# Another hand-written order for a linear-attention and MLP kernel on one core

## The chip, the cores and the metric

The kernel runs on one core of one Trainium2 chip. The metric is device time in microseconds (us) of one execution, lower is better. TensorE is called PE here, VectorE DVE, ScalarE ACT, GpSimd POOL and the sync engine SP, as in the profile.

## The reference

Two parts follow each other. The first is attention with decay over blocks of tokens, for 4 batches, 8 heads, 768 tokens and head dimension 64; the second is an MLP on its output, 3072 tokens by 512.

```python
# attention, per batch and head, block after block
intra = einsum('bhic,bhjc->bhij', qb, kb) * Dmask      # lam ** (i - j) for i >= j
intra = einsum('bhij,bhjd->bhid', intra, vb)
inter = einsum('bhid,bhde->bhie', qb * lam_pow, kv_state)
out[:, :, sl] = intra + inter
kv_state = lam_block * kv_state + einsum('bhsd,bhse->bhde', kb * rev_pow, vb)
# MLP, d_model 512, d_ff 2048
h = x @ w_in
g = where(h >= 1, h, where(h <= -1, 0, (h + 1) ** 2 / 4))
return g @ w_out
```

## The kernel before

The 3072 tokens are cut into eight stripes, `STRIPES` on line 28: per batch two pieces, of 4 and 2 blocks of 128 tokens in the first batch and of 3 and 3 in the others. Stripes are numbered 0 to 7. In each, the eight heads are worked on as four pairs, 0 to 3. Nothing is scheduled by a planner at run time or at build time: the kernel is one loop over the words of the string `ORDER` (lines 32 to 74), and each word emits a few instructions. Each engine runs its own instructions strictly in the order in which the words stand, and waits in place where an operand or a buffer isn't ready. So the list sets which instruction waits behind which, on five engines and on two queues that issue transfers: SP's for q, k, v and the results, POOL's for the weights.

The words, with stripe `s` and head pair `p` as the first two digits:

- `L s half c`: load one half of the heads of q, k or v of a stripe (SP, lines 159 to 165). Stripe 0 is loaded in quarters, two heads at a time. `W0` to `W3` load four column blocks of the first weight (line 234), `W4` to `W7` four row blocks of the second (line 238), both on POOL's queue, where the numbers are turned to bf16. `@X` after either makes its first transfer wait until the load `X` has landed.
- `k`, `q`, `v` with a last letter: the decayed k and q and the cast of v, from f32 to bf16 (lines 294 to 319). The last letter is the engine: `a` ACT, `g` POOL, `d` DVE. A k on POOL or ACT is two instructions, on DVE one.
- `T`, `Q`: transposes of k and q, on PE for stripes 0 to 3 (line 343), by a transfer on SP for stripes 4 to 7 (line 335). `t`, `u`: ACT copies them out.
- `S`: scores on PE, `s`: mask on DVE. `R`: products of k and v on PE, `r`: state update on DVE. `b`: the last state of stripe 0 copied into a block-diagonal tile for stripe 1; `z`: decayed k copied into a tile with zero columns. `O`: output on PE (it needs the `s` and the `r` of its pair, in stripe 1 also its `b`), `o`: ACT casts it out. For stripes 4 to 7 `X` transposes it by a transfer on SP.
- `P s n`: one of 16 column blocks of the first matmul (line 594), `K`: the same for blocks 0 to 2 of stripe 0, k-slice by k-slice (line 608); `h`: Relu on ACT (line 617). `A s a`: the rest of the activation on DVE, three instructions over four blocks (lines 574 to 576). `Y s m a`: a quarter of the second matmul for 128 tokens (line 626), which needs `A s a` and weight block `W(4+a)`. `y` copies the result, `U` stores it, `Z72` does all of that for the last 128 tokens (line 646).
- `J`: the zero columns of the tiles `vc`, `kz` and `bd` are cleared on POOL (lines 263 and 265). `E`: a table for the state of stripe 0 on POOL. `B`: mask tables. `G`: zero columns of the tiles of stripes 4 and 5. `D n`: n matmuls of the identity on PE, which no result uses (line 582).

The buffers for q, k and v hold two stripes each, so a load of stripe s waits for the casts of stripe s - 2. Five tiles hold decayed k and q (`kq`).

The order of the start in the list before, engine by engine: SP issues q, k, v of stripe 0 in the order q0 k0 k2 k1 q1 k3 v0 q2 q3 v1 v2 v3, then L10q. POOL does J, k02, E, q03, W0, v02, W1, W2, W3, q11, q10, W4. L10v, L10k and what follows on SP waits for W1 to land. The main loop:

```python
for word in order(NS):
    word, _, dep = word.partition("@")
    ...
    if dep:
        after(dmas[word][0], dmas[dep][-1])
```

Of the kernel before, what the change touches and what calls it, by code (L numbers as in the profile page):

```python
# [38 lines left out]
P09 h08 u10 k13d P0d k11a W6 h0a z13d h09 T10 P0c q13g L20q@W4 b10d T11 v11a t10 P0b S10 s10
z11a W7 z12d P0e t11 h0c R11 Q13 S11 D1 P0f L20v h0b r11 h0d T13 b12a q12d h0f s11 A01 h0e Q12  # L40
T12 A02 t13 Y000 v10a Y020 Y010 Y030 u13 L21q u12 Y031 R10 r10 L30q t12 Y011 Y001 Y021 A03 v12a
k23g Y022 Y012 k21d O11 S12 Y032 v13a R12 o11 s12 Y033 q21g Y023 q20g R13 Y013 k20a r13 r12 S13
O12 y02 s13 o12 Y002 y01 q23g q22g O10 O13 Y003 z21a L30k y03 o10 o13 Q20 P12 P11 u20 T20 h12
P13 t20 Q21 k22d T21 h11 v21d y00 z20d v20d R20 P10 P18 S20 P15 h10 h13 u21 r20 t21 P17 k30g s20
Q22 P19 h18 T22 A10 S21 h19 q30d u22 t22 P16 O20 s21 h17 o20 P14 R21 P1b Q23 T23 h16 L31q h14
z22g k31g P1d S22 L21v@W2 r21 s22 h15 P1e U02 U03 h1b O21 h1d L31k u23 P1a o21 P1c t23 h1a q31g
L31v z23g T30 Q30 q33g P1f u30 v22a Y110 L30v S23 T31 h1c A11 t30 Q31 G40 h1e q32g k32g Y100 R22
A12 t31 Y101 Y111 u31 v23a R23 r22 Y102 h1f s23 r23 S30 O22 O23 s30 k33d z33g o22 Y112 Q32 z30d
z32d T32 z31d v33a v32d v31g A13 o23 t32 G42 u32 P25 T33 h25 P20 S31 v30a P21 Y103 h21 R30 h20
P24 r30 P23 R31 y10 L40k s31 G41 P22 h23 h22 h24 Q33 P26 L40v S32 G43 r31 U00 Y113 h26 P2f P27  # L50
L40q t33 G50 u33 k41d h2f h27 R33 y11 A20 P2e r33 s32 P2b q41g O31 A21 k42a h2e P28 P29 q40g O30
P2a h2b h29 P2c o30 h2a R32 S33 h2c v41d r32 v40a o31 P2d q42g O32 Y200 s33 L50k R41 o32 h28 O33
Y201 o33 P32 P33 L50q h2d k50a h33 v43d A22 P31 k40d h32 q43a Y202 P30 R40 q50g h31 A23 P39 h30
P3a h3a h39 Y210 P36 Y203 T41 A30 h36 P37 y20 T40 S40 s40 h37 Y211 P34 P3e r40 S41 T42 L50v r41
P3d v42g h3e P38 s41 k43g R42 T43 h34 h38 O40 P3b L60q P3c k52g S42 o40 h3d R43 v50g k51a h3b
r42 P35 Y212 s42 r43 S43 O41 P3f s43 Y213 h35 o41 R50 q53a U10 L60k T50 O43 o43 h3c Y220 O42
# [685 lines left out]
```

## Time and profile before

| | us |
|---|---|
| median of 3 runs | 223.96 (223.47 to 226.75) |
| the profiled execution: its time | 224.02 |
| its span in the profile | 222.3 |
| PE busy | 211.4 |
| DVE busy | 155.6 |
| ACT busy | 127.3 |
| POOL busy | 59.7 |

The span is what the profile shows between the first and the last instruction; the 1.7 us beside it lie outside the program's own instructions. A busy PE is a PE with a matmul in flight. In the views quoted below, a timeline row gives the start, the length, the engine, the line, and in brackets how long the engine was idle before it and what ended that. A row of the table by stretches gives for each engine its busy time and, in brackets, its instructions, then PE's granted clock, the share of the transfer engines and GB/s.

### The profile page before, as it was taken

The page shows a single profiled execution, that of the slowest core. Times are in us where ns is not written, and L with a number is a line of the kernel's source. Part 1 is how long each engine was busy: PE and PEld are TensorE (multiplying, and loading weights), DVE is VectorE, ACT ScalarE, POOL GpSimd, SP SyncE. Part 2 cuts the span into 40 slices and gives each one's busy share as a digit, 9 for nine tenths or more (in the row PEclk, how much of TensorE's full clock was granted, in tenths as well). Part 3 has the DMA queues.
Part 4 walks back from the last instruction along what each step waited for, and adds up shares of the span by engine and source line. Part 5 has one row for each costly group of instructions (what it writes and reads, how often), then busy time and mean ns, then how long its engine had stood idle before and what let it go on. Part 6 is the DMA issues. An engine that isn't in the chain of part 4 may idle for free.

```text
span 222.3 us, 4425 instructions
## 1 busy us (share of the span) xinstructions
PE 211.4 (95%) x1675; PEld 121.3 (55%) x1675; DVE 155.6 (70%) x242; ACT 127.3 (57%) x276; POOL 59.7 (27%) x107
## 2 busy tenths in 40 slices
PE   7488999999999899999999999999999999999994
PEld 2245444445875456555654566556565565455543
DVE  6497058964899979898797659948967496307900
ACT  2758499326894668775671776337563564174520
POOL 8446036004592336260353020211610000000000
PEclk9999999999999999999999999999999999999999
DMA  5999999999999999059996999799646103122112
GB/s 124 245 243 152 205 197 177 199 209 232 274 248 228 242 205 196 3 95 221 260 158 163 162 258 255 130 214 201 169 84 165 47 1 86 35 86 104 47 50 94
DMA packets 100629, 35.95 MB, mean 162 GB/s; under 512 B 89216, under 2 KB 97664, under 8 KB 100608
## 3 DMA queue, kind: packets, MB, share of 16 engines
q1 hardware_dynamic: 96384, 31.47, 65.9%
q0 software_dynamic: 4224, 4.19, 12.1%
q8 instruction: 13, 0.21, 0.4%
q14 instruction: 8, 0.07, 0.1%
HBM read 27.27 MB, written 6.29 MB: 151 GB/s over the span
## 4 chain that ended last, share of the span: by engine, by line
PE 75%; DMA 9%; SPq 5%; issue 4%; DVE 4%; POOL 1%; ACT 0%; POOLq 0%; DVEq 0%
PE py L626 33%; PE ph L594 30%; DMA k_nat<-in_k_dram 4%; DMA w_in_sb<-in_moe_w_in_dram 3%; SPq L163 2%; PE ps L367 2%; DMA q_nat<-in_q_dram 2%; SPq L165 2%; PE py L646 2%; PE pk L448 1%; PE po L512 1%; PE ph L608 1%; DVE tt L575 1%; PE po L531 1%; PE pt L343 1%
## 5 line engine op out<-in xcount | busy, mean ns | idle before, releaser
L617 ACT ACTIVATE tt<-ph,one 128x384 bf16<-128x384 f32 (+2 forms) x128 | 70.1, 586 | 39.0 <-PE ph L594 28.9
L594 PE MATMUL ph<-xT,w_in_sb 128*128 128x384 bf16 (+2 forms) x500 | 92.2, 325 | 0.0
L626 PE MATMUL py<-w_out_sb,gT 128*128 128x512 bf16 x368 | 87.4, 379 | 1.2 <-DVE gT L576 1.2
L594 PEld LDWEIGHTS <-w_in_sb 128*128 128x128 bf16 x500 | 46.5, 98 | 29.4 <-issue 0.2
L626 PEld LDWEIGHTS <-gT 128*128 128x128 bf16 x368 | 34.3, 98 | 36.0 <-DVE gT L576 1.6
L574 DVE TENSOR_SCALAR mm<-tt 128x1536 bf16<-128x1536 bf16 (+2 forms) x32 | 19.1, 597 | 22.5 <-ACT tt L617 21.7
L388 DVE TENSOR_TENSOR sc<-ps,mask 128x768 bf16<-128x768 f32 (+1 forms) x28 | 25.6, 915 | 11.7 <-PE ps L367 10.3
L576 DVE TENSOR_TENSOR gT<-tt,mm 128x1536 bf16<-128x1536 bf16 (+2 forms) x32 | 32.7, 1023 | 1.2
L575 DVE TENSOR_TENSOR tt<-tt,mm 128x1536 bf16<-128x1536 bf16 (+2 forms) x32 | 32.1, 1004 | 1.1
L314 POOL TENSOR_SCALAR kq<-k_nat,dec 128x192 bf16<-128x192 f32 (+2 forms) x30 | 20.6, 698 | 29.1 <-PE ps L371 14.7
L634 ACT COPY osb<-py 128x512 f32<-128x512 f32 x23 | 13.5, 586 | 21.2 <-PE py L626 19.9
L319 POOL TENSOR_TENSOR kq<-q_nat,dec 128x384 bf16<-128x384 f32 (+2 forms) x18 | 17.3, 975 | 20.6 <-DMA q_nat<-in_q_dram 9.4
L476 DVE SCALAR_TENSOR_TENSOR sz<-sz,lam_blk,pk 128x128 bf16<-128x128 bf16 x48 | 16.6, 346 | 6.7 <-PE pk L448 5.4
L296 POOL CAST vc<-v_nat 128x384 bf16<-128x384 f32 (+1 forms) x9 | 6.4, 712 | 29.4 <-PE po L531 19.5
L343 PE MATMUL pt<-ident,kq 128*128 128x128 bf16 x96 | 9.4, 220 | 3.5 <-ACT kq L310 2.1
L294 ACT CAST vc<-v_nat 128x384 bf16<-128x384 f32 (+2 forms) x15 | 7.4, 502 | 7.3 <-DMA v_nat<-in_v_dram 7.3
L549 ACT CAST xT<-po 128x384 bf16<-128x384 f32 (+2 forms) x16 | 7.5, 483 | 6.9 <-PE po L526 5.9
L582 PE MATMUL pw<-ident 128*128 128x512 bf16 x31 | 9.8, 432 | 1.4 <-POOL ident masks.py:199 1.4
L343 PEld LDWEIGHTS <-kq 128*128 128x128 bf16 x96 | 6.7, 98 | 7.5 <-ACT kq L310 3.4
L351 ACT COPY kqT<-pt 128x384 bf16<-128x384 bf16 (+2 forms) x16 | 7.8, 490 | 3.4 <-PE pt L343 3.3
L547 ACT CAST xn<-po 128x384 bf16<-128x384 f32 x16 | 7.7, 480 | 3.2 <-PE po L531 3.2
L353 ACT COPY kqT<-pt 128x384 bf16<-128x384 bf16 (+2 forms) x16 | 7.6, 486 | 0.9 <-PE pt L343 0.9
(78 smaller groups left out, 163.6 us busy)
## 6 DMA issues: line engine op xcount, KB each, us to landing
out_dram<-osb SPq DMA_DIRECT2D x23, 256.0 KB, 2.6
q_nat<-in_q_dram SPq DMA_DIRECT2D x18, 256.0 KB, 4.6
k_nat<-in_k_dram SPq DMA_DIRECT2D x24, 128.0 KB, 4.3
v_nat<-in_v_dram SPq DMA_DIRECT2D x24, 128.0 KB, 4.4
k_nat<-in_k_dram SPq DMA_DIRECT2D x12, 256.0 KB, 4.9
v_nat<-in_v_dram SPq DMA_DIRECT2D x12, 256.0 KB, 4.5
w_in_sb<-in_moe_w_in_dram POOLq DMA_DIRECT2D x4, 512.0 KB, 9.1
w_out_sb<-in_moe_w_out_dram POOLq DMA_DIRECT2D x4, 512.0 KB, 8.9
```

Source lines behind the costliest of these rows:

```text
L314: nc.gpsimd.tensor_scalar(dst[:, hi, :, :], src[:, hi, :, :], dec[:, row, 2 * hp + hi:2 * hp + hi + 1], 0.0, AX.mult, AX.add)
L319: (nc.gpsimd if eng == "g" else nc.vector).tensor_tensor(dst, src, decay(row, 2 * hp, C, inner), op=AX.mult)
L343: nc.tensor.transpose(out=d["pt"][:, i, c, :], in_=d["kq"][:, i * C + c, :], identity=ident)
L388: nc.vector.tensor_tensor(out=d["sc"][:, :, 0:C, :], in0=d["ps"][:, :, 0:T].rearrange("p h (c i) -> p h c i", c=C), in1=_ins(mask[:, 2 * h ...
L476: nc.vector.scalar_tensor_tensor(out=d["ss"][:, c, :], in0=prev, scalar=lam_blk[:, hp:hp + 1], in1=kv, op0=AX.mult, op1=AX.add)
L574: nc.vector.tensor_scalar(mm, tt, 0.5, 1.0, AX.mult, AX.min)
L575: nc.vector.tensor_tensor(tt, tt, mm, op=AX.subtract)
L576: nc.vector.tensor_tensor(g[:, 4 * a:4 * a + 4, 0:T], tt, mm, op=AX.mult)
L594: nc.tensor.matmul(ph[:, 0:T], lhsT=w_in_sb[:, ko, ni * 128:(ni + 1) * 128], rhs=x_tiles[s][:, ko, 0:T], start=(ko == 0), stop=(ko == KO - 1))
L617: nc.scalar.activation(out=t_tiles[s, ni // 4][:, ni % 4, 0:T], in_=p_tiles[s, ni][:, 0:T], func=AF.Relu, bias=one[:, 0:1])
L626: nc.tensor.matmul(y_tiles[s, m], lhsT=g_tiles[s][:, ko, m * 128:(m + 1) * 128], rhs=w_out_sb[:, ko, :], start=(ko == 0), stop=(ko == FO - 1))
L634: nc.scalar.copy(out=osb, in_=y_tiles[s, m])
```

## The change

Only `ORDER` changes; nearly every word stands elsewhere. The functions, the stripes and the buffers stay, and the line numbers behind the list grow by one. The first words of both lists:

```diff
-D2 D1 D2 D2 D2 D2 J D2 L00q L00k D1 L02k B1a q00d k00a T00 t00 L01k L01q q01d k02g L03k k03d D2
-D1 B0a T02 k01a L00v D1 Q00 D2 L02q u00 T01 S00 t01 s00 L03q Q01 D1 u01 D2 q02d S01 Q02 T03 s01
-E L01v D2 v00a R00 t02 v01d R01 q03g r00 W0 r01 L02v L03v u02 Q03 t03 v02g W1@L01k L10q S02 D2
-O00 u03 s02 R02 L10v@W1 v03a R03 B2a W2@L01v O01 W3 L10k@W1 S03 q11g r02 q10g o01 D1 r03 L11k
-W4@L10v s03 O02 o00 O03 L11q@W2 B3a o02 o03 L11v@W4 Q10 D1 K01 P03 K00 k10g K02 h03 K03 Q11 h00
...
+D1 D1 D1 D1 D1 D1 D1 D1 L03q L00q D1 L00k L01q q00g k00a D1 q01d D1 D1 D1 L01k L00v L02k Q00
+L01v D1 Q01 L02q D1 u00 T00 t00 D1 D1 k01d v00d q03g S00 D1 s00 E q02g L02v W0 L03k D1 u01 k02a
+T01 R00 v01d D1 t01 L03v D1 k03g W1@L03q D1 W2 L10q T02 R01 q10g B0a B2a S01 r01 v02a D1 D1 Q03
+s01 Q02 D1 t02 D1 D1 u02 D1 B3a D1 q11g S02 D1 v03a T03 t03 L10k@W0 u03 R02 B1a D1 r00 J R03
+W3@L01q s02 r02 b12g k11g D1 O00 o00 r03 S03 O01 o01 L11k@W0 L10v@W2 O02 D1 o02 s03 O03 Q11 K01
+o03 K00 P03 h03 K02 W4@L00q K03 h00 L11q k13g L20q@W3 P06 h02 Q10 k12g h01 P04 u11 P07 u10 A00
...
```

Engine by engine, where the prediction needs it. SP: the start is q3 q0 k0 q1 k1 v0 k2 v1 q2 v2 k3 v3, L10q; then L10k and L11k wait for W0, L10v waits for W2, and L11q, L20q@W3, L11v@W4, L20k, L20v@W6, L21q, L21k, L30q, L21v@W6 follow. POOL: q00, q03, E, q02, W0, k03, W1, W2, q10, q11, J, W3, b12, k11, W4, k13, k12, W5, W6, z10, W7, v12, k21, q20, q21. DVE before the second activation of stripe 0: A00 k10 q12 v11 s10 r11 q13 v10 s11 b10 b13 r10 s12 A01 (before: A00 k13 z13 b10 s10 z12 r11 q12 s11 A01). PE before the first `Y`: ... P0f R10 S12 O11 O10 Y000 (before: P0f T13 Q12 T12 Y000). DVE before the fourth activation of stripe 1: s22 A12 s23 r22 r23 A13 (before: A12 r22 s23 r23 s30 k33 z33 z30 z32 z31 v32 A13, with z33 on POOL). The end is Y713 Z72 (before: Y713 D1 Z72).

Over the whole list the casts are spread otherwise: POOL has 71 words in place of 61, DVE 125 in place of 129, ACT 246 in place of 252. The `D` matmuls are 33 in place of 31. All other matmuls, transposes, transfers and activations are the same in number and size.

More of the change, by code (lines that the diff above doesn't have):

```diff
@@ L39 @@
[L39 to L56, printed above, removed]
@@ new lines @@
+L01v D1 Q01 L02q D1 u00 T00 t00 D1 D1 k01d v00d q03g S00 D1 s00 E q02g L02v W0 L03k D1 u01 k02a
[3 more added lines that the diff above has]
+o03 K00 P03 h03 K02 W4@L00q K03 h00 L11q k13g L20q@W3 P06 h02 Q10 k12g h01 P04 u11 P07 u10 A00
+P0b h06 L11v@W4 L20k@W0 h04 h0b P08 h07 P0a P05 b11a T11 h08 W5 k10d T10 P0d P09 h0a W6 t11 t10
@@ new lines @@
+q12d v11d S10 P0e h05 s10 z11a R11 z10g T12 P0c r11 q13d t12 W7 h0e v12g S11 v10d s11 T13 Q13
+z12a Q12 u13 P0f u12 L20v@W6 t13 k21g h09 L21q h0c h0f R10 b10d L21k@W3 S12 b13d r10 q20g O11
+O10 q21g s12 Y000 o10 h0d Y030 S13 A01 Y020 Y010 q22g Y001 z13d L30q Y031 Y021 Y011 L21v@W6 A02
+Y032 q23g o11 A03 v13a Y012 k23g Y002 Y022 L30k R12 R13 r12 Y023 k20a y02 r13 s13 Y013 O13 O12
+v20d k22g o13 Y033 o12 T20 Q20 L31k y01 P10 z20d y03 P12 R20 t20 v23g L31q h10 z21d v21d u20 P13
+r20 P11 S20 h13 h11 T21 Q21 P15 P14 s20 h12 O20 u21 z23g P16 k30g t21 h14 A10 R21 S21 P19 h15
@@ new lines @@
+o20 h19 P17 Q22 u22 Y003 h17 r21 s21 h16 q30d P1f P1a k31g P18 h1f P1d U03 q31g T23 T22 Q23 h18
+h1a y00 z22d t22 P1b A11 P1e P1c O21 h1b S22 o21 t23 Y100 u23 q33g L30v q32g h1e L31v Q30 T30
+u30 Y101 T31 z31g v22a t30 L40q s22 S23 Q31 Y110 t31 A12 R22 Y102 u31 s23 R23 r22 Y111 r23 S30
+O22 h1c h1d A13 k33g O23 o22 Y112 o23 k32a T33 U01 v31g z33d t33 R31 P27 G40 P23 U00 r31 L50q
+z32d z30a Q33 L40k v33a G41 Y113 v30g T32 G42 s30 h23 Q32 u33 v32g G50 G43 q42g R33 k41g y11 P22
+h27 t32 q41a L40v r33 S31 u32 h22 P20 P21 s31 h20 h21 R32 R30 r32 S32 r30 k40g Y103 s32 P26 P25
@@ new lines @@
+v51a A32 Y300 Y222 h3d k53g X41 r52 Y301 X42 Y321 Y223 X43 R50 Y302 q52d Y322 P43 R51 A33 y22
+P42 Y303 s50 r51 Y323 S51 v53g U10 T53 T52 r50 h43 y32 s51 L60k P47 q62g P40 O51 h42 P4a h40 S52
+k60g L60v o51 O50 h47 h4a s52 y30 q60a P4b R53 P41 P46 S53 r53 h41 q61a P45 Y310 h45 Y311 U22
+k61a k63d A40 P44 h4b O52 v62g P48 s53 q63g o50 U30 h46 h44 P49 O53 h48 P4d T60 o52 X51 T61 X50
+v63a v60g o53 P4c X52 h4c X53 Y312 Y313 S60 P4f k62d v61g y31 P4e R60 h49 Y410 A41 s60 U32 h4e
+Y400 A42 r60 h4d R62 h4f P53 Y411 A43 T62 r62 T63 h53 Y401 L70q q71g Y402 q73g q70g S61 U31 P51
@@ L74 @@
+h69 P6c s73 o70 h66 h6b Y520 U21 A62 O73 o72 X72 h6c Y521 X70 o73 A61 P6f h6f X73 Y522 Y610 Y600
+Y601 Y523 h6e P70 Y611 y52 P73 h73 Y602 P72 Y612 h70 A63 P71 Y603 Y613 h71 P76 y60 h72 P79 U50
+y61 h79 P78 P75 P77 h78 h75 U52 h77 P74 A70 P7d h76 P7b h74 P7a P7e h7b h7a U51 A71 h7e Y620 P7f
+Y621 U61 U60 P7c Y622 A72 Y623 h7c h7f h7d Y710 Y711 A73 Y700 Y701 Y712 y62 Y702 Y703 Y713 y70
+U62 U70 y71 U71 Z72
 """
```

30 lines of the change are left out of this document (12 added, 18 removed).

## The prediction

> **What bounds the kernel now.** I read the page's head first, then busy time by stretches, then the waits of PE, then the timeline at the places where PE stands.
>
> ```profile
> span 222.3 us, 4425 instructions
> PE 211.4 (95%) x1675; PEld 121.3 (55%) x1675; DVE 155.6 (70%) x242; ACT 127.3 (57%) x276; POOL 59.7 (27%) x107
> ```
>
> ```profile
> core 0: us, PE busy (x) PEld busy (x) DVE busy (x) ACT busy (x) POOL busy (x), PEclk, DMA share, GB/s
> 22.40:70.00 47.60, 47.53 (x365) 26.85 (x366) 32.54 (x51) 32.55 (x80) 17.86 (x29) 1.00 1.07 218
> 70.00:80.00 10.00, 8.32 (x79) 4.72 (x77) 8.51 (x17) 4.65 (x10) 2.15 (x8) 1.00 1.06 226
> 80.00:90.00 10.00, 10.00 (x93) 6.40 (x91) 9.79 (x14) 7.86 (x17) 5.74 (x6) 1.00 0.92 183
> 90.00:100.00 10.00, 9.88 (x82) 5.75 (x77) 9.05 (x15) 7.33 (x17) 4.89 (x5) 1.00 0.29 54
> 100.00:215.00 115.00, 115.00 (x850) 66.01 (x849) 80.11 (x123) 60.51 (x123) 16.05 (x21) 1.00 0.68 138
> ```
>
> ```profile
> PE py L626 <- DVE gT L576: 1.2, 1, 1.2
> ```
>
> From 22.4 us to the end PE is without a matmul for 0.07 + 1.68 + 0.12 = 1.87 us only, at a full clock. The list neither adds nor drops MLP or attention matmuls. So the kernel's time is the moment when the first MLP matmul starts, plus PE's fixed work, plus the holes in it. A new list can win the 1.87 us of holes and whatever the start gives; it can lose without bound.
>
> ```profile
> 13.12 0.68 DVE L319 TENSOR_TENSOR kq<-q_nat,dec 128x512 bf16<-128x512 f32 x1
> 13.83 1.06 POOL L319 TENSOR_TENSOR kq<-q_nat,dec 128x512 bf16<-128x512 f32 x1 [4.77 <-DMA q_nat<-in_q_dram]
> 14.83 0.96 POOL L234 DMA_DIRECT2D w_in_sb<-in_moe_w_in_dram  x1
> 16.68 2.23 POOL L234 DMA_DIRECT2D w_in_sb<-in_moe_w_in_dram  x3
> 21.55 0.58 ACT L549 CAST xT<-po 128x512 bf16<-128x512 f32 x1 [0.46 <-PE po L537]
> 22.39 0.82 PE L608 MATMUL ph<-xT,w_in_sb 128*128 128x512 bf16 x3 [0.45 <-DMA w_in_sb<-in_moe_w_in_dram]
> 24.90 0.37 SPq L165 DMA_DIRECT2D v_nat<-in_v_dram  x1
> ```
>
> The start is a chain: q03 on POOL waits for its load, W0 is issued behind it at 14.83, and the first MLP matmul waits for W0 until 22.39. The attention of stripe 0 is ready just before, at 21.55 + 0.58 = 22.13.
>
> **The start: +0.1 us.** POOL now meets q02 ahead of W0 in place of q03. In both lists that load is SP's fifteenth issue (lam and 13 others ahead) with the same eight quarters, 256 KB each, in front. So I expect it at 13.8, the cast until 14.9 and W0 at 14.83 as before. What moves: q02 was a DVE cast, done at 13.80, and is now POOL's, done at 14.89, 1.1 us later. If all of that reached the last xT cast, it would end at 23.2. Only P03 reads that tile, and it stands behind K01 and K00, six matmuls from 22.39 on at 0.82 for three, until 24.0; but PE reaches K01 only after O03, so up to 0.4 us can show. Faster is possible only if W0 and the attention both come sooner: 0.3 at most, since the attention has no reason to. Bounds -0.3 to +0.4.
>
> **Transfers from 22 to 50: nothing directly.** Both halves of stripe 1's k are now issued when W0 lands, while W1 and W2 are in the queue; W3 stands behind J. J's price is in the old start:
>
> ```profile
> 3.22 1.07 POOL L263 MEMSET vc<- 128x256 bf16 x4
> 5.04 0.64 POOL L265 MEMSET bd<- 128x128 bf16 x4
> ```
>
> That is 3.22 to 5.68, 2.5 us, then idle; now it runs behind q11, at about 20 us, so W3 is issued near 23 us in place of 18.2. Who is served first?
>
> ```profile
> q0 software_dynamic: 407, 0.41, 122.6%
> q1 hardware_dynamic: 24, 0.01, 1.5%
> ```
>
> These are the two queues from 26 to 28 us: v and k, issued from 24.90 on, got 1.5% while the weights issued by 18.9 took everything. Transfers are served about in the order of issue. So k cannot push W1 (landed at 24.90, first read at about 26) or W2. W3 shares with 0.5 MB of k and lands at an estimated 31.5, first read (P0d) near 32.9. Cost 0, cover 1.4 us.
>
> In return W4 is no longer behind L10v:
>
> ```profile
> 30.00:32.00 2.00, 2.00 (x11) 0.88 (x9) 1.50 (x2) 1.56 (x4) 0.65 (x1) 1.00 0.82 181
> 32.00:34.00 2.00, 2.00 (x13) 0.84 (x11) 0.72 (x3) 2.00 (x6) 1.91 (x5) 1.00 0.83 165
> 50.00:52.00 2.00, 2.00 (x19) 1.00 (x18) 1.52 (x5) 0.85 (x2) 0.24 (x1) 1.00 0.97 254
> ```
>
> The transfer engines were at 0.82 against 1.2 under a full queue, about 1.3 us of transfer lost, which the new list uses. It shows in the next step but one.
>
> **O10 behind the state copies: +0.8 us.**
>
> ```profile
> 33.91 0.73 DVE L427 COPY bd<-ss 64x64 bf16<-64x64 bf16 x2
> 36.46 0.35 DVE L476 SCALAR_TENSOR_TENSOR sz<-bd,lam_blk,pk 128x128 bf16<-128x128 bf16 x1
> 37.06 0.68 DVE L388 TENSOR_TENSOR sc<-ps,mask 128x512 bf16<-128x512 f32 x1
> 37.66 0.68 DVE L574 TENSOR_SCALAR mm<-tt 128x2048 bf16<-128x2048 bf16 x1
> 38.38 1.23 DVE L575 TENSOR_TENSOR tt<-tt,mm 128x2048 bf16<-128x2048 bf16 x1
> 39.64 1.23 DVE L576 TENSOR_TENSOR gT<-tt,mm 128x2048 bf16<-128x2048 bf16 x1
> ```
>
> S11 stands at the same place on PE, one P before the last, so s11 ends near 37.8 again. Then DVE does b10, b13 and r10: 0.73 + 0.73 + 0.35 = 1.8, until 39.6. PE has R10, S12, O11 and then O10, which needs r10, at about 38.8. It waits 0.8 us (0 if s11 comes that much sooner, 1.8 if PE is there when s11 ends). A01 is late next: s12 0.69, then 0.68 + 1.23 + 1.23 gives 43.5. Its first reader Y001 stands five words after Y000 (four Y at 0.86 and S13), at 39.6 + 0.3 + 3.7 = 43.6. It just fits, so nothing on top.
>
> **Q20 behind k21 on POOL: +0.3 us.**
>
> ```profile
> 49.59 0.56 DVE L319 TENSOR_TENSOR kq<-k_nat,dec 128x384 bf16<-128x384 f32 x1 [2.03 <-DMA k_nat<-in_k_dram]
> 51.76 0.83 POOL L314 TENSOR_SCALAR kq<-k_nat,dec 128x192 bf16<-128x192 f32 x2 [14.71 <-PE ps L371]
> 52.90 1.64 POOL L319 TENSOR_TENSOR kq<-q_nat,dec 128x384 bf16<-128x384 f32 x2 [0.31 <-DMA q_nat<-in_q_dram]
> 54.59 0.34 PE L343 MATMUL pt<-ident,kq 128*128 128x128 bf16 x3
> ```
>
> Before, Q20 started at 54.59, just as q20's cast ended. L21k had landed at 49.59. Now L20q, L20v and L21q, 1.18 MB, go ahead of it: 4.7 us at the 254 GB/s of the stretch from 50 to 52, less the 1.3 us regained and about 0.5 from L11v's shorter wait, so 52.5. POOL casts k21 (0.83) and only then q20 (0.82): 54.2. PE is there at 54.59, less 0.86 since Y003 now comes later, plus the 0.9 so far: 54.6. No wait at these numbers, but little cover, and each us by which L21k is later is a us of PE. I take 0.3; bounds 0 to 3.
>
> **The hole at 78 us: -1.6 us.**
>
> ```profile
> 64.19 1.51 DVE L574 TENSOR_SCALAR mm<-tt 128x1024 bf16<-128x1024 bf16 x1
> 73.37 0.55 DVE L319 TENSOR_TENSOR kq<-k_nat,dec 128x384 bf16<-128x384 f32 x1
> 73.84 0.86 DVE L414 COPY kz<-kq 128x384 bf16<-128x384 bf16 x3
> 74.62 1.72 DVE L296 CAST vc<-v_nat 128x384 bf16<-128x384 f32 x1
> 76.26 0.41 DVE L574 TENSOR_SCALAR mm<-tt 128x1024 bf16<-128x1024 bf16 x1
> 78.18 1.04 PE L626 MATMUL py<-w_out_sb,gT 128*128 128x512 bf16 x4 [1.22 <-DVE gT L576]
> ```
>
> PE stands 1.22 us for A13, which DVE starts at 76.26 because k33, three z copies and v32 are in front: 2.9 us from 73.37 on. The new list has them behind A13, or on POOL and ACT. A13 then ends near 75.2 while its first reader comes at 77, so 1.22 us go, and about 0.4 of the other holes between 70 and 80. Bounds -1.7 to 0. What is late next is the casts put behind A13, for stripe 3.
>
> **The end: -0.2 us.** The identity matmul ahead of Z72 is gone; it stands on the path:
>
> ```profile
> 215.67 0.22 PE pw L582
> ```
>
> The two added `D` fill waits at the start and cost nothing.
>
> **The rest: +0.4 us.** From 80 us on PE had 0.12 us of holes, so nothing is to be won there, and every cast, transpose and store has another place. The old list lost 1.9 us in 200, one place in all; I put a quarter of that on the new one, with 0 to 1.9 as bounds.
>
> Sum on the profiled execution's 224.02, which is 0.06 above the median: 0.1 + 0.8 + 0.3 - 1.6 - 0.2 + 0.4 = -0.2, so 223.8.
>
> **Rivals.** *Slower: POOL's queue at stripe 2.* If L21k lands at 55 rather than 52.5 (the old list had its loads held by a full queue there), k21 and q20, slowed by DVE as the rows of 64.19 against 76.26 show DVE slowed by POOL, end at 57.2 and Q20 waits 2.6 us; z21, which needs k21, then holds DVE up too, and the hole at A13 comes back in part, 0.5. 223.8 - 0.3 + 2.6 + 0.5 = 226.6. It decides from L21k at 52.9 on. For it: the cover is 0.4 us. Against: the early weights free the queue. Chance 0.27.
>
> *A13 stays late.* POOL has ten casts more, and beside POOL the same instruction took 1.51 in place of 0.41. If three such meetings fall on A11 to A13, 3.3 us of DVE time eat the 2.9 won, and the hole stays: 223.8 + 1.6 = 225.4. Against: the moved work also leaves DVE. Chance 0.18. The Trainium skill, SBUF — State Buffer, section "Who interferes with whom", speaks for it: GpSimd and a DVE instruction with two SBUF inputs or in a two-port mode share a port pair, held for a whole instruction. By that rule the rows just quoted agree, and more casts on POOL cost DVE.
>
> *k takes half of the transfer engines from W1.* If the two queues took turns, 0.5 MB of k at 22.4 would delay W1, 2.5 us of transfer behind W0, by up to 2.1 us, to 27.0; P06 reads it near 25.9, so 1.1 us lost: 224.9. The row of 1.5% speaks against it. Chance 0.08. The Trainium skill, DMA: Bandwidth & Descriptors, section "SWDGE vs HWDGE vs iDMA", says that software and hardware descriptor generation feed different queues of an engine, which goes round among them. By that rule this rival would hold; this case's 26 to 28 us do not agree with it.
>
> *Faster: no new hole.* Without the waits at O10 and Q20, and with the old holes gone, 224.02 - 1.87 - 0.22 = 221.9. For it: both waits are worked out with fractions of a us. Chance 0.12.
>
> *The forecast* keeps 0.35.
>
> **How the numbers follow.** The likeliest is 223.8, its own range 222.8 to 225.0. Signs are mixed, so the range reaches to the fast rival at 221.9 and past the slow one at 226.6: 221.9 to 227.2. Over 2% (4.5 us, about what a measurement of this kernel can tell from no change) faster would be below 219.5, under the floor of 221.9 unless the start moves by 2.4 us: 0.02. Over 2% slower, above 228.4, takes the slow rival at its bound and a second hole: 0.08. Within 2%: 0.90.
>
> **What would show it.** Right: the first MLP matmul at 22.2 to 22.8 behind W0; a wait of PE for line 476 or 427's DVE work just before the second matmul starts near 39; no wait over 0.3 us for A13 near 76. The slow rival would show as PE waiting for a POOL cast of q near 55. The forecast is wrong as a whole if W0 is issued more than 0.5 us away from 14.8, if PE waits for w_in at any block but the first, or if PE has more than 1 us of holes after 100 us.

## The result and the profile after

The changed kernel takes 220.93 us (median of four runs, 220.52 to 221.41), the kernel before 223.72 (223.4 to 226.75): a ratio of 0.988, 95% interval 0.985 to 0.992. The forecast was 223.8 with a range from 221.9: it was too slow by 2.9 us, and the range missed by 1.0. The profiled execution of the changed kernel took 221.41 us. Medians and ranges in this document are of all runs, while the ratios and their intervals leave out slow runs, such as the one of 226.75 us here.

First the page's head, the busy time by stretches and the waits of PE, all after:

```profile
span 219.5 us, 4436 instructions
PE 211.5 (96%) x1677; PEld 122.0 (56%) x1677; DVE 148.1 (67%) x239; ACT 126.3 (58%) x270; POOL 63.6 (29%) x120
```

```profile
30.00:40.00 10.00, 8.79 (x70) 4.30 (x69) 6.81 (x16) 8.24 (x21) 5.64 (x11) 1.00 0.97 181
70.00:80.00 10.00, 10.00 (x105) 6.05 (x102) 7.86 (x19) 7.71 (x18) 3.34 (x11) 1.00 0.97 234
80.00:90.00 10.00, 10.00 (x90) 6.68 (x88) 8.83 (x12) 8.33 (x19) 6.42 (x8) 1.00 0.71 136
90.00:210.00 120.00, 120.00 (x890) 69.06 (x888) 85.97 (x129) 64.63 (x132) 17.35 (x23) 1.00 0.70 141
```

```profile
PE py L627 <- DMA w_out_sb<-in_moe_w_out_dram: 1.2, 1, 1.2
```

PE's work is the same (211.4 before). The stretch from 70 to 80 us, where PE was busy for 8.32 us before, is full; the wait for line 576's DVE work is not in the list any more. A new hole of 1.2 us stands between 30 and 40. So one hole went and one came, and yet 2.6 us were won in this pair of profiles. Part of the rest is at the start:

```profile
14.15 0.96 POOL L235 DMA_DIRECT2D w_in_sb<-in_moe_w_in_dram  x1
21.61 1.46 PE L609 MATMUL ph<-xT,w_in_sb 128*128 128x512 bf16 x6
```

W0 is issued at 14.15 instead of 14.83, and the first MLP matmul starts at 21.61 instead of 22.39.

To see all of it I took the starts of PE's matmuls one after the other. A hole is what lies between two starts beyond the first one's length (its columns at 2.4 per ns and 2.5 ns, which gives the usual distance of two starts in these traces, 216 ns for 512 columns and 56 for 128). The start of the last matmul is then the start of the first MLP matmul plus the holes plus fixed work: 192.79 us in the list before, 192.36 in the new one, which has two identity matmuls (0.43 us) less behind that point. By this definition the sum comes out exactly; it needs every matmul's record, and these four traces have them all (1675 and 1677):

| kernel | first MLP matmul | holes to 40 us | 40 to 70 | 70 to 90 | later | last matmul |
|---|---|---|---|---|---|---|
| before | 22.39 | 0.72 | 0.68 | 2.27 | 0.32 | 219.16 |
| after | 21.61 | 1.86 | 0.28 | 0.18 | 0.03 | 216.32 |
| old list again | 21.05 | 1.05 | 0.37 | 2.11 | 0.01 | 217.38 |
| new list again | 21.75 | 0.70 | 0.33 | 0.12 | 0.78 | 216.04 |

The two lower rows are the same two kernels run once more (below). They turn the reading of the start round: the old list can start at 21.05, earlier than the new one.

### The profile page after: what moved, and what is told of

Same layout as the page of the kernel before. It is cut to its first block, busy times and chain, and to the rows that moved or that the text cites. A ratio compares the mean times of both kernels' runs of the same rounds, so it can differ in the third digit from the quotient of the medians.

```text
span 219.5 us, 4436 instructions
## 1 busy us (share of the span) xinstructions
PE 211.5 (96%) x1677; PEld 122.0 (56%) x1677; DVE 148.1 (67%) x239; ACT 126.3 (58%) x270; POOL 63.6 (29%) x120
## 4 chain that ended last, share of the span: by engine, by line
PE 81%; DMA 13%; SPq 4%; POOL 1%; issue 1%; DVE 0%; POOLq 0%; DVEq 0%
PE py L627 36%; PE ph L595 32%; DMA w_out_sb<-in_moe_w_out_dram 4%; DMA k_nat<-in_k_dram 4%; DMA w_in_sb<-in_moe_w_in_dram 3%; SPq L164 3%; PE ps L368 2%; DMA q_nat<-in_q_dram 2%; PE pk L449 2%; PE py L647 2%; PE po L506 1%; PE pt L344 1%; PE po L513 1%; PE ps L372 1%; PE po L532 1%; SPq L160 1%
## 5 line engine op out<-in xcount | busy, mean ns | idle before, releaser
L627 PEld LDWEIGHTS <-gT 128*128 128x128 bf16 x368 | 34.5, 98 | 36.2 <-DMA w_out_sb<-in_moe_w_out_dram 1.4
L577 DVE TENSOR_TENSOR gT<-tt,mm 128x1536 bf16<-128x1536 bf16 (+2 forms) x32 | 31.6, 988 | 1.2
L575 DVE TENSOR_SCALAR mm<-tt 128x1536 bf16<-128x1536 bf16 (+2 forms) x32 | 19.6, 611 | 18.1 <-ACT tt L618 17.0
L315 POOL TENSOR_SCALAR kq<-k_nat,dec 128x192 bf16<-128x192 f32 (+2 forms) x34 | 19.2, 578 | 31.2 <-DMA k_nat<-in_k_dram 31.1
L320 POOL TENSOR_TENSOR kq<-q_nat,dec 128x384 bf16<-128x384 f32 (+2 forms) x20 | 18.2, 929 | 24.6 <-DMA q_nat<-in_q_dram 21.6
L297 POOL CAST vc<-v_nat 128x384 bf16<-128x384 f32 (+1 forms) x15 | 10.6, 715 | 35.1 <-DMA v_nat<-in_v_dram 20.3
L583 PE MATMUL pw<-ident 128*128 128x512 bf16 x33 | 11.0, 450 | 1.4 <-POOL ident masks.py:199 1.4
L295 ACT CAST vc<-v_nat 128x384 bf16<-128x384 f32 (+2 forms) x8 | 4.2, 528 | 10.0 <-DMA v_nat<-in_v_dram 10.0
L352 ACT COPY kqT<-pt 128x384 bf16<-128x384 bf16 (+2 forms) x16 | 7.6, 483 | 3.3 <-PE pt L344 3.3
L311 ACT ACTIVATE kq<-k_nat,dec 128x192 bf16<-128x192 f32 (+1 forms) x16 | 6.8, 465 | 2.9 <-DMA k_nat<-in_k_dram 2.6
```

Of the source, the lines that this page charges most:

```text
L315: nc.gpsimd.tensor_scalar(dst[:, hi, :, :], src[:, hi, :, :], dec[:, row, 2 * hp + hi:2 * hp + hi + 1], 0.0, AX.mult, AX.add)
L320: (nc.gpsimd if eng == "g" else nc.vector).tensor_tensor(dst, src, decay(row, 2 * hp, C, inner), op=AX.mult)
L575: nc.vector.tensor_scalar(mm, tt, 0.5, 1.0, AX.mult, AX.min)
L577: nc.vector.tensor_tensor(g[:, 4 * a:4 * a + 4, 0:T], tt, mm, op=AX.mult)
L627: nc.tensor.matmul(y_tiles[s, m], lhsT=g_tiles[s][:, ko, m * 128:(m + 1) * 128], rhs=w_out_sb[:, ko, :], start=(ko == 0), stop=(ko == FO - 1))
```

## The experiments

### Both lists again, and where J stands

Every kernel here differs from one of the two lists in its words alone, unless its edit says otherwise. The first suspicion was a row of before that the prediction hadn't weighed. The timeline of before, then of the first execution after:

```profile
2.17 3.53 DVE L187 TENSOR_SCALAR pos<-pos_i 128x10 f32<-128x10 int32 x1
6.11 0.29 ACT L199 ACTIVATE dec<-ex 128x104 f32<-128x104 f32 x1 [1.94 <-DVE ex L196]
```

```profile
2.16 0.25 DVE L188 TENSOR_SCALAR pos<-pos_i 128x10 f32<-128x10 int32 x1
4.39 0.29 ACT L200 ACTIVATE dec<-ex 128x104 f32<-128x104 f32 x1 [0.33 <-DVE ex L197]
```

A conversion of ten columns lasts 3.53 us before and 0.25 after, and the decay table, which every decayed k and q reads, comes 1.7 us later. While it lasted POOL ran J's memsets, which the new list has behind q11. So J alone was moved, in both directions.

```diff
 e1 (new list)
-D1 D1 D1 D1 D1 D1 D1 D1 L03q ... D1 r00 J R03
+D1 D1 D1 D1 D1 D1 D1 D1 J L03q ... D1 r00 R03
 e2 (old list)
-D2 D1 D2 D2 D2 D2 J D2 L00q ... q11g r02 q10g o01
+D2 D1 D2 D2 D2 D2 D2 L00q ... q11g r02 q10g J o01
```

> The new list with one word moved: J stands ahead of the first load again. Theory A, the cleared columns: while POOL clears them, DVE's conversion of the positions is held (3.53 us before, 0.25 us after), the decay table is 1.7 us later, and with it the attention of stripe 0 and the first MLP matmul: the conversion takes about 3.5 us again, the first MLP matmul stands at 22.2 to 22.4 us in place of 21.6, the time is 221.6. Theory B, the loads: the first MLP matmul follows W0, and W0 follows the load of q02, which J doesn't touch: the conversion is long again, W0 is issued at 14.15, the first MLP matmul stays at 21.6 and the time at 220.9. Either way the wait for W4 near 38 us stays, or shrinks as W3 and what stands behind it on POOL come 2.5 us sooner.

> The old list with one word moved: J stands behind the cast q10, as in the new list. Theory A: the conversion falls from 3.53 to 0.25 us, the decay table is ready at 4.7 in place of 6.4, the first MLP matmul comes at 21.6 to 21.8 in place of 22.4, the time falls by 0.7 to 223.0. Theory B: the same conversion, but q03's load still lands at 13.8, W0 is issued at 14.8, the first MLP matmul stays at 22.3 and the time at 223.6.

Measured: e1 220.88 us (220.04 to 222.8), ratio 0.992 (0.989 to 0.995), as fast as the new list, with a conversion of 0.25 us though J's memsets ran from 3.25 on. e2 222.73 (221.97 to 224.56), ratio 1.000 (0.997 to 1.003). J's place moves neither list's time. Then both lists were run again, unchanged:

> The old list once more, unchanged. In its first profile DVE's conversion of the positions took 3.53 us; in four other lists, two of them with the old list's first words, it took 0.25. Theory C, a disturbance of that one execution: the conversion takes 0.25 us here, the decay table is ready at 4.5 in place of 6.4, q03 lands near 13.1, W0 is issued near 14.1 and the first MLP matmul stands at 21.0 to 21.3; the median is again near 222.9. Theory A', a property of the old program: 3.5 us again, W0 at 14.8, the first MLP matmul at 22.4, the time near 223.9. Either way the hole at A13 near 76 us is there (1.2 us or more).

> The new list once more, unchanged, on the same chip as the runs beside it: first MLP matmul at 21.6, a wait of 1.2 us for W4 near 38 us, no other hole above 0.3; 220.9. If the gain seen first was in part the disturbed start of the old list's runs, the distance to the old list here is 1.9 to 2.2 us rather than 2.8.

Measured: the old list 222.5 (221.68 to 229.41), its profiled execution 222.3; the new one 220.86 (220.36 to 221.46), its profiled execution 221.22. The timeline of the old list this time:

```profile
2.16 0.25 DVE L187 TENSOR_SCALAR pos<-pos_i 128x10 f32<-128x10 int32 x1
4.54 0.29 ACT L199 ACTIVATE dec<-ex 128x104 f32<-128x104 f32 x1 [0.33 <-DVE ex L196]
14.05 0.97 POOL L234 DMA_DIRECT2D w_in_sb<-in_moe_w_in_dram  x1
```

The same program has a short conversion in one execution and a long one in another. The start of 22.39 us on which the prediction was built is that of one execution; run again, the old list starts at 21.05.

### What holds the conversion

In the long ones the end tells: 2.17 + 3.53 = 5.70 us, and POOL's last memset (the row of 5.04 in the prediction) ends at 5.68. Theory L: a small DVE conversion that meets POOL's memsets waits until POOL's unbroken run is over. To make it meet them, the small cast ahead of it is repeated, in both lists.

```diff
     nc.vector.tensor_copy(pos[:, 0:Q4], pos_i[:, 0:Q4])
+    nc.vector.tensor_copy(pos[:, 0:Q4], pos_i[:, 0:Q4])
+    nc.vector.tensor_copy(pos[:, 0:Q4], pos_i[:, 0:Q4])
+    nc.vector.tensor_copy(pos[:, 0:Q4], pos_i[:, 0:Q4])
     nc.vector.tensor_scalar(pos[:, Q4:NR], pos_i[:, Q4:NR], 1.0, 0.0, AX.add, AX.add)
```

> Old list; ahead of the conversion of line 187 (pos from int32 to f32 on DVE) the small cast of line 186 is written three times more, so that the conversion starts some 0.3 us later, after POOL's memset of lam_z has begun at 2.33 us. Theory L (a DVE conversion that meets POOL's memset is held until POOL's unbroken run of memsets ends; in the two long executions it ended at 5.70 and 5.72, the memsets of bd at 5.68 and 5.69): one of these small DVE instructions lasts until about 5.7 in this execution and in every other, the decay table comes at 6.1, the first MLP matmul at 22.4 instead of 21.05, and the median is 223.5 to 223.9, a ratio of 1.00 to 1.005. Rival (the long conversion comes from something before the program, at random): conversion 0.25, first MLP matmul at 21.05, median 222.5 as for the old list again.

> New list with the same three casts. J is not in POOL's first run there. Theory L: the DVE instruction is held only until the memset of lam_z ends, about 3.3, ahead of the logarithm at 3.9 to 4.3, so the decay table stays at 4.4 to 4.8, the first MLP matmul at 21.6 to 21.8 and the median at 220.9 (220.6 to 221.2): J's new place costs nothing where the race is lost, and 1.3 us are saved against the old place. Rival: a held conversion is held for 3.5 us whatever stands in POOL's run; then the start is about 1.3 us later and the median near 222.2.

The timelines, old list first (of an execution of 230.07 us, of which only the first 6 us are used):

```profile
2.10 3.60 DVE L187 CAST pos<-pos_i 128x3 f32<-128x3 int32 x1
2.33 0.95 POOL L207 MEMSET lam_z<- 128x1024 f32 x1
5.03 0.64 POOL L268 MEMSET bd<- 128x128 bf16 x4
```

```profile
2.10 1.20 DVE L188 CAST pos<-pos_i 128x3 f32<-128x3 int32 x1
2.34 0.95 POOL L208 MEMSET lam_z<- 128x1024 f32 x1
```

A cast of three columns is held until 5.70 where J follows the memset of `lam_z` (POOL ends at 5.67), and until 3.30 where nothing follows it (3.29). So the hold is shown, and that it ends with POOL's run. Six more traces agree: the conversion lasts 3.55 us in e5 below, where J stands in its old place, and 1.14 or 1.15 in e6, e9, e10, e11 and e12, where nothing follows `lam_z`. Times: old 223.03 (221.65 to 230.07), ratio 0.999 (0.996 to 1.002); new 221.45 (220.48 to 224.08), ratio 0.990 (0.985 to 0.994). Each lies between its two forecasts. So the counter-experiment: POOL begins its memsets only when the conversion is done.

```diff
+    scr = const.tile([128, 1], F32, name="scr")
+    nc.gpsimd.tensor_copy(scr, pos[:, NR - 1:NR])
     nc.gpsimd.memset(lam_z, 0.0)
```

> Old list; ahead of the memset of lam_z POOL copies one column of pos into a scratch tile, so that its memsets start only when DVE's conversion is done. If holds explain the old list's median of 223.3 to 223.5 against 222.3 for an execution without one: conversion 0.25, decay table at 4.5 to 4.7, first MLP matmul at 21.05 to 21.2, median 222.3 to 222.6, a ratio to the old list near 0.995. Rival (holds are rare or are made up for later in most executions): the profile looks the same, but the median stays within 0.3 us of the old list's in the same batch.

> New list with the same copy on POOL. With J behind the first stripe's casts a hold ends at 3.3, before the logarithm of lam, so there is nothing to win: 220.8 to 221.2, as the new list, by either theory. A median under 220.5 would say that holds cost the new list too.

Measured: the old list 223.18 (222.26 to 227.16), ratio 1.001 (0.999 to 1.003); the new one 220.88 (220.56 to 221.18), ratio 0.991 (0.989 to 0.993). The rival is right: without a hold the old list's median is what it was. Whether holds are rare or are made up for later, this doesn't tell. Timeline and waits of the old list without a hold:

```profile
2.16 0.26 DVE L187 TENSOR_SCALAR pos<-pos_i 128x10 f32<-128x10 int32 x1
2.60 0.95 POOL L206 MEMSET lam_z<- 128x1024 f32 x1
```

```profile
PE py L628 <- DVE gT L578: 1.2, 1, 1.2
PE pt L345 <- POOL kq L321: 1.1, 1, 1.1
```

Its first MLP matmul is at 21.36, a microsecond earlier than in the execution of before, and PE then stands 1.1 us, from 35.4 on, for a transpose that waits for POOL's cast of q. In this execution the stretch to 40 us takes back what the start wins: the second matmul starts at 38.35, in the one of before at 38.41. The hole at A13 (1.2 us) is there as ever.

### What the start is worth at 40 us

Two hybrids have the words up to K01 from one list and the rest from the other; words that would then stand twice are left out, and those that would be missing are put in ahead of K01.

```diff
 e3 (old list from K01 on)
-D2 D1 D2 D2 D2 D2 J D2 L00q ... Q10 D1 K01
+D1 D1 D1 D1 D1 D1 D1 D1 L03q ... W4@L00q ... Q10 ... K01
 e4 (new list from K01 on)
-D1 D1 D1 D1 D1 D1 D1 D1 L03q ... s03 O03 Q11 K01
+D2 D1 D2 D2 D2 D2 J D2 L00q ... Q10 D1 b12g k11g Q11 K01
```

> The new list up to the first MLP matmul, then the old list's words in the old order (with W4 behind k11, without a wait for L10v). If the two parts of the gain are separate, the start is that of the new list (first MLP matmul at 21.6) and the holes after it are those of the old list (about 4.0 us start to start, with the one of 1.4 at A13): 223.7 - 0.8 = 222.9. If the holes follow from the loads of the start, which come in another order and behind W0, they change too: above 224 if they grow, near 221 if they go.

> The old list up to the first MLP matmul, then the new list's words in the new order. If the parts are separate: first MLP matmul at 22.4, the holes at 50 to 100 us of the old list (2.8 us) gone, the wait for W4 as W4 lands in the old list (none), 0.4 us of identity matmuls gone: 223.7 - 2.8 - 0.4 = 220.5 with the wait for W4 gone, 221.7 with it. If the new holes depend on the new loads of the start, new waits appear near 50 us and the time is above 222.5.

| kernel | first MLP matmul | holes to 40 us | 40 to 70 | 70 to 90 | later | last matmul |
|---|---|---|---|---|---|---|
| e3: new start, old rest | 22.36 | 1.28 | 0.52 | 1.70 | 0.90 | 219.43 |
| e4: old start, new rest | 21.65 | 1.46 | 0.28 | 0.17 | 0.03 | 215.84 |
| e2: old list, J moved | 21.04 | 0.69 | 0.60 | 2.01 | 0.02 | 217.15 |
| e1: new list, J back | 21.65 | 1.39 | 0.33 | 0.25 | 0.03 | 216.02 |

Measured: e3 224.81 (224.32 to 225.47), ratio 1.010 (1.007 to 1.014); e4 221.92 (220.79 to 225.59), ratio 0.996 (0.992 to 0.999). The stretch from 70 to 90 goes with the rest of the list, not with the start. The starts themselves are not the parents' (22.36 against the new list's 21.61 and 21.75; 21.65 against the old list's 21.05), and why e3 is slower than both lists stays open.

Now add the first two columns: where the work stands at 40 us. Old list 23.11, 22.10 and 21.73 (before, again, e2); new list 23.47, 22.45 and 23.04 (after, again, e1). The new one is 0.7 us behind in the mean, and each list varies by more than that. Part of the old list's spread goes with the hold. The trace of e5 (below), which has the old list's words up to 70 us, has a hold too:

```profile
2.17 3.55 DVE L188 TENSOR_SCALAR pos<-pos_i 128x10 f32<-128x10 int32 x1
```

It stands at 22.58 + 0.28 = 22.86 us. So the two executions with a hold are at 23.11 and 22.86, the two without at 22.10 and 21.73; f3's, without one, was as late as before's. In e5 W0 is issued at 13.91, so there the hold doesn't delay W0; what is late is the attention of stripe 0, whose last xT cast starts at 22.35 (20.82 in the old list run again). What put W0 at 14.83 in the first profile stays open.

What comes behind 40 us adds 3.27, 2.49 and 2.63 in the old list, 0.49, 1.23 and 0.61 in the new one: 2.0 us less in the mean, and 0.43 for the identity matmuls. 2.0 + 0.4 - 0.7 = 1.8 us, with rounding (1.1 to 2.8 in the three pairs). The medians differ by 2.8 us at first, by 2.6 between the new list run again and the 28 runs of the old one beside it (median 223.46), and by 1.6 between the two lists run again (222.5 and 220.86). Three pairs of traces can't tell more than that the account is of that size.

### The hole at 78 us

In the old list A13 alone is moved ahead of the casts of stripe 3.

```diff
 e5 (old list)
-A12 t31 Y101 Y111 u31 v23a R23 r22 Y102 h1f s23 r23 S30 ... v33a v32d v31g A13 o23
+A12 t31 Y101 Y111 u31 v23a R23 r22 Y102 h1f s23 r23 A13 S30 ... v33a v32d v31g o23
```

> The old list with one word moved: A13 stands right behind r23, ahead of s30, k33, the z copies and v32 on DVE. Theory 1, DVE's order at A13 is the largest part of the gain: the hole near 76 us goes (1.4 us from start to start), nothing else changes, 222.9 - 1.4 = 221.5, or 221.2 if the small holes at 70 to 73 us go too. Theory 2, the holes move: s30, k33 and v32 are 1.8 us later, PE waits for them at S31, T33 or R32 soon after, and the time stays within 0.4 of 222.9.

Measured: 222.0 us (221.54 to 226.24), ratio 0.994 (0.992 to 0.997), beside an old list at 223.46 (222.5 run again). The timelines of DVE and PE in e5:

```profile
72.22 0.69 DVE L577 TENSOR_TENSOR gT<-tt,mm 128x1024 bf16<-128x1024 bf16 x1
72.83 0.95 DVE L389 TENSOR_TENSOR sc<-ps,mask 128x768 bf16<-128x768 f32 x1
74.30 0.34 PE L344 MATMUL pt<-ident,kq 128*128 128x128 bf16 x3 [0.44 <-DVE kq L320]
```

A13 ends at 72.91, some 5 us sooner than before, and its hole is gone. But s30 and k33 now come behind it, and T33 waits for that k: holes between 70 and 90 fall from 2.1 to 1.08 us, not to 0.2. Then three edits together: J behind q10, A13 behind r23, and no identity matmuls behind K01.

> Old list with three edits only: J behind q10, A13 behind r23, and no identity matmuls behind K01. If the change's gain is these three (no long hold at the start, 1.4 us of hole at A13 of which 0.6 comes back as another wait, 0.43 us for two identity matmuls), an undisturbed execution takes about 222.3 - 0.8 - 0.4 = 221.0, and the median is 220.9 to 221.3, within 0.3 us of the new list. If much of the gain lies in the other hundreds of moved words, it stays above 221.7.

Measured: 221.66 (221.15 to 221.95), ratio 0.992 (0.989 to 0.995). The new list had 0.988 at first, 0.989 run again and 0.991 in f4, so three edits give two thirds of its gain or more. T33's wait of 0.81 us at 73 is the largest hole of e10 behind 40 us; the new list has none, since k33 is POOL's there and its z copies are POOL's, ACT's and DVE's.

### How the two queues share the transfer engines

The new hole after is W4's. The timeline after:

```profile
21.32 3.88 SPq L166 DMA_DIRECT2D k_nat<-in_k_dram  x4
30.25 0.91 POOL L315 TENSOR_SCALAR kq<-k_nat,dec 128x128 bf16<-128x128 f32 x2 [7.77 <-DMA k_nat<-in_k_dram]
31.12 0.80 POOL L239 DMA_DIRECT2D w_out_sb<-in_moe_w_out_dram  x1
39.51 1.68 PE L627 MATMUL py<-w_out_sb,gT 128*128 128x512 bf16 x7 [1.21 <-DMA w_out_sb<-in_moe_w_out_dram]
```

W4 has no wait of its own any more, but on POOL it stands behind k11, which waits 7.77 us for k; so it is issued at 31.12, only 0.23 us sooner than before, and PE can use it 8.4 us later, where it took 7.0 us to land before. Moved right behind W3, at 22.32:

```diff
 e6 (new list)
-W3@L01q s02 r02 ... K02 W4@L00q K03
+W3@L01q W4@L00q s02 r02 ... K02 K03
```

> The new list with one word moved: W4 is issued right behind W3, ahead of b12 and k11, which waits for its load until 30 us. Theory 1, served in the order of issue: W4 lands near 32, the wait of 1.2 us at the first second-layer matmul goes, and k10 and k11, 0.5 MB that share with one more weight block, land up to 2.5 us later, at 32 to 33, which T11 and T10 (near 31 us) show as a wait of 1 to 2 us: 219.6 to 221.5. Theory 2, k is not held up (it is issued at 21.3, W4 at 22.6): no wait at T11, 219.6.

Measured: 223.33 (222.32 to 224.69), ratio 1.000 (0.997 to 1.003), 2.5 us slower than the new list. The waits of PE and the timeline of e6:

```profile
PE pt L344 <- POOL kq L315: 1.8, 1, 1.8
```

```profile
32.53 0.92 POOL L315 TENSOR_SCALAR kq<-k_nat,dec 128x128 bf16<-128x128 f32 x2 [8.92 <-DMA k_nat<-in_k_dram]
```

With W4 in front k comes 2.3 us later, and T11's hole is 1.95 us. The other way round, W3 behind k:

```diff
 e11 (new list)
-W3@L01q s02 r02 b12g k11g
+W3@W1 s02 r02 b12g k11g
```

> New list with W3 waiting for W1, so that it is issued near 25 instead of 21.2, behind the four transfers of the second stripe's k. Served in the order of issue: k lands 1.5 to 2 us sooner (28.5 to 29 instead of 30.2 to 30.6), the 0.64 to 0.73 us for which PE waits at T11 near 31 goes, W4 is issued near 29.5, and W3, which lands near 31.5 as the last of the same bytes, is still in time for P0d near 32.9: median 220.2 to 220.4. Rival (the queues share): k lands as before and W3 late, PE waits for w_in at P0d for 1 us or more: 221.5 or over.

Measured: 220.31 (219.88 to 221.71), ratio 0.990 (0.986 to 0.993), with 219.93 in the profiled execution: the fastest of all kernels here, though beside f4's 220.88 in the same batch its gain over the new list is within the intervals. The timeline:

```profile
23.66 0.81 POOL L235 DMA_DIRECT2D w_in_sb<-in_moe_w_in_dram  x1 [2.40 <-DMA w_in_sb<-in_moe_w_in_dram]
27.64 2.87 POOL L315 TENSOR_SCALAR kq<-k_nat,dec 128x128 bf16<-128x128 f32 x2 [2.63 <-DMA k_nat<-in_k_dram]
38.16 1.04 PE L627 MATMUL py<-w_out_sb,gT 128*128 128x512 bf16 x3
```

k lands 2.6 us earlier, T11 has no hole (though k11's cast lasts 2.87 us here, for a reason that stays open), no wait for W3 or W4 is left, and PE reaches the second matmul at 38.16 instead of 39.51.

Both results were expected of service in the order of issue, but the packets in the traces show something else. In the execution of before no packet of v or k moves for 2.9 us after the first of them was issued at 24.90:

```profile
q0 software_dynamic: 599, 0.60, 124.1%
```

That is the whole list of queues with traffic from 24.9 to 27.8 us; q0 carries the weights, and by 28 us they are nearly through. So the prediction's row of 1.5% from 26 to 28 us covers mostly this delay, and can't tell an order of issue from turns. At this place, where the weights fill the engines, the first packet of k or v comes 2.9 to 3.7 us after its issue in 17 of the 18 traces (2.0 in f1); late in the kernel, without weights, stores and transposing transfers need 0.8 to 1.2. And there are stretches in which the two queues take turns. This is e6 from 26 to 31 us:

```profile
q0 software_dynamic: 796, 0.80, 93.7%
q1 hardware_dynamic: 736, 0.18, 27.8%
```

There are nearly as many packets of one as of the other (796 and 736), but a weight's packet carries 1.0 KB and one of k 0.25, so k gets about a fifth of the bytes there. It isn't so everywhere: after, from 24 to 26 us, k's queue moved 423 packets and the weights' 329. This fits both edits: W4 behind W3 leaves weights beside k for longer, and W3 behind W1 lets k go through nearly alone (1513 packets of k beside 98 of the weights from 24.7 to 26.5 us).

Last, two mixed lists that take the old, earlier start. e12 differs from e9 in its transfers.

```diff
 e9 (from e4)
-J ... q11g r02 q10g o01 D1 r03 L11k ... k11g Q11 K01 K00 P03 h03 K02 K03 h00
+... q11g r02 q10g J o01 D1 r03 L11k ... k11g K01 K00 P03 h03 K02 K03 Q11 h00
 e12 (from e9)
-L10v@W1 v03a R03 B2a W2@L01v O01 W3 L10k@W1 S03 q11g r02 q10g J o01 D1 r03 L11k W4@L10v
+v03a R03 B2a W2@L01v O01 L10k@W0 S03 q11g r02 q10g J W3@W1 o01 D1 r03 L11k L10v@W2 W4@L00q
```

> The old start up to K01 with J moved behind q10, then the new list's rest, with Q11 behind K03 as the old list has it. If the start term is what the undisturbed executions show (21.05 old, 21.6 to 21.75 new) and the holes of the rest are the new list's (1.9 us), the first MLP matmul is at 21.05 to 21.1 and the median at 220.2 to 220.4, a ratio near 0.985 to 0.988, with no execution near 224 from a held conversion. Rival: the rest fits only its own start, so an earlier first matmul comes back as waits for weights or k between 30 and 40 us (T11 waited 1.06 us for k behind the old start): then 220.8 to 221.2.

> The mixed list (old start with J behind q10, new rest, Q11 behind K03) with k issued when W0 has landed, W3 behind W1 and v of stripe 1 behind k. If T11's 1.69 us of waiting in the mixed list are the late k and k now lands near 28.5, the start of 21.2 is kept: holes fall from 3.2 to about 1.5 us between 30 and 40, and the median is 219.7 to 220.2, below the new list. Rival: something else comes due in that window (v for v11, W3 for P0d) and the sum of start and holes stays what it is: 220.8 to 221.4.

Measured: e9 221.34 (220.96 to 223.75), ratio 0.992 (0.988 to 0.995); e12 222.77 (221.33 to 224.34), ratio 1.000 (0.996 to 1.003). Both started early, at 21.22 and 21.39. Their waits, e9 first:

```profile
PE pt L344 <- POOL kq L315: 1.5, 1, 1.5
```

```profile
PE pk L449 <- DVE vc L297: 2.9, 1, 2.9
36.18 0.43 DVE L320 TENSOR_TENSOR kq<-q_nat,dec 128x256 bf16<-128x256 f32 x1 [6.31 <-DMA q_nat<-in_q_dram]
36.52 0.29 DVE L297 CAST vc<-v_nat 128x256 bf16<-128x256 f32 x1
```

In e9 T11 waits for k11's cast, which POOL starts at 31.52, behind W4 (which waits for v) and b12, though k landed at 30.68. In e12 k is early, and R11 stands 2.9 us for v11's cast, which DVE has behind q12: v lands at 35.4 and q at 36.2, where e9 had q at 35.2. Here W4 was issued at 24.66, ahead of v and q. As mechanisms both rivals hold, but e12's time is above either of its forecasts. In these two lists the earlier first matmul is lost again by 40 us to late transfers and to what stands behind them; the old list without a hold (22.10 and 21.73 at 40 us) keeps it, so this is no rule.

## Why the prediction was wrong

*The frame* (start, fixed work and holes) is exact as a sum, but its terms aren't independent: what the start wins, waits for transfers up to 40 us can take back, as in f3, e9 and e12. I priced them one by one. In the first pair of profiles the terms came out as start -0.8 us, holes to 40 us +1.1 (W4), 40 to 70 -0.4, 70 to 90 -2.1, later -0.3, identity matmuls -0.4.

*The start, +0.1.* Fails, and with it the test I had set, W0 within 0.5 us of 14.8: it went at 14.15. The step that failed is the base: 14.83 and 22.39 were taken as the list's, and were those of one execution, with a long conversion and a late W0; the old list issued W0 at 14.05 when run again and 14.03 in e2. The path fails with it: after, the first MLP matmul doesn't wait for W0 at all (the row of 21.61 has no wait). Between executions without a hold the new list starts 0.7 us later (21.75 against 21.05), between the two first profiles 0.8 earlier.

*Transfers, 0, and W4 freed.* W3 came in time; k didn't push W1, but not for the reason given: its first packet came at 24.65, when W1 had landed at 23.4. "W4 no longer behind L10v" overlooked what else stands ahead of W4 on POOL: k11, which waits for k until 30.25. Its hole is 1.37 us in one execution (8.4 us from issue to use) and nothing in the other, where W4, issued at 31.45, was there by 38.51. The rule from the Trainium skill that I had made a rival of (DMA: Bandwidth & Descriptors, section "SWDGE vs HWDGE vs iDMA", queues served in turn) agrees with the traces in such stretches, if the turns are counted in packets. From 26 to 28 us after, with both queues full:

```profile
q0 software_dynamic: 309, 0.32, 92.8%
q1 hardware_dynamic: 297, 0.08, 28.7%
```

SP's queue, with k, moved 297 packets beside 309 of the weights, and a quarter of their bytes. Still no matmul waited for w_in.

*O10 behind the state copies, +0.8.* Mis-sized by nearly all of it. The timelines of DVE and PE after:

```profile
35.98 0.67 DVE L389 TENSOR_TENSOR sc<-ps,mask 128x512 bf16<-128x512 f32 x1
36.57 0.80 DVE L428 COPY bd<-ss 64x64 bf16<-64x64 bf16 x4
37.41 0.35 DVE L477 SCALAR_TENSOR_TENSOR sz<-bd,lam_blk,pk 128x128 bf16<-128x128 bf16 x1
38.03 0.22 PE L527 MATMUL po<-kqT,bd 128*128 128x128 bf16 x1
```

s11 (the row of 35.98) ended at 36.65, not 37.8, and the four copies took 0.80 in all, where I had put 0.73 for each pair. r10 ends at 37.76 and O10 follows at 38.03: no hole of note.

*Q20 behind k21, +0.3.* Not there:

```profile
50.22 0.83 POOL L315 TENSOR_SCALAR kq<-k_nat,dec 128x192 bf16<-128x192 f32 x2 [1.05 <-DMA k_nat<-in_k_dram]
51.03 1.63 POOL L320 TENSOR_TENSOR kq<-q_nat,dec 128x384 bf16<-128x384 f32 x2
53.58 0.50 PE L344 MATMUL pt<-ident,kq 128*128 128x128 bf16 x6
50.55 1.60 SPq L166 DMA_DIRECT2D k_nat<-in_k_dram  x3
```

The step took the wrong load. k21 is head pair 1 and reads the first half of the heads, L20k; L21k, the second half, is issued at 50.55 only (the last row), when k21's cast runs already. L20k stands ahead of L20v, L21q and L21k in the new list: its last transfer landed by 50.03 (49.40 before), 2.5 us ahead of my 52.5, and of the transfers charged to it L20q had landed by 34.6 and L20v and L21q stood behind it. q20 and q21 are done at 52.66, ahead of PE. The slow rival at stripe 2, which was given 0.27, rests on the same slip and fell with it.

*The hole at 78 us, -1.6.* Right in place and cause, and the largest real term: 2.27 to 0.18 us between 70 and 90 in the first pair, 2.11 to 0.12 in the second. e5 shows that the order on DVE is its cause, and that the move alone, with the casts behind A13 still on DVE, leaves 1.08 us of holes there.

*The end, -0.2.* The direction is right, the count is not: two identity matmuls left the path, not one (the old list has another near 36.9), 0.43 us in place of 0.22.

*The rest, +0.4.* Wrong in the first pair, where the new list has 0.28 us between 40 and 70 and 0.03 behind 90 (the old one 0.68 and 0.32); run again it had one hole of 0.73 at 139, where PE waited for a transposing transfer. So the term is real, but belongs to single executions.

Without the four charges (0.1, 0.8, 0.3 and 0.4) the sum would have been 222.2, near the rival "no new hole" (221.9), which got 0.12; the measured 220.93 is below that too. The 0.8 us that the start won in the first pair is luck: the profile of before has a late one. Of the losses, the 0.8 took s11's end from the old list, though the new order itself moves it, and the 0.3 took the wrong load. What stays open: why the holes up to 40 us differ by up to 1.2 us between executions of one list, how often the hold comes and what it costs in the median, and so how the 1.6 to 2.8 us between the medians divide among the terms.

## What to carry to other kernels

Before a sum is built on a profile, look for an instruction that lasts many times longer than its like: 3.53 us for ten columns was in the timeline, and a base that holds a chance event misleads. Run the base twice. Where transfers fill a window, price a start and the waits behind it together; check for each cast which load it reads, and look at what else stands ahead of an issue on its engine. Here a hole closed by moving one word (A13) came back by half, because the work behind it stayed on that engine.
